# Loading q and k of the first two token groups together: 1 KB packets, a borrowed buffer, and interleaved attention at the start of a fused attention and FFN kernel

## The chip, the cores and the metric

The kernel runs on one core of a Trainium2 chip. A core has five engines that run side by side: TensorE (PE in the profile, with its weight loads as PEld), VectorE (DVE), ScalarE (ACT), GpSimd (POOL) and SyncE (SP), which here mostly issues DMAs. Sixteen DMA engines move data between the chip's main memory and the core's SBUF. PE writes its results to PSUM, from where DVE and ACT copy them to SBUF.

The metric is the device time of one execution in microseconds. The kernel before took 280.76 us, the median of four runs (280.69 to 281.13).

## What is computed

Attention inside chunks of 64 tokens, then a feed-forward block with a squared ReLU. Batch 8, 8 heads, 576 tokens, head dimension 64; so 4608 tokens of width 512, and a hidden width of 2048.

```python
scores = scale * np.matmul(q_c, k_c.transpose(0, 1, 2, 4, 3))   # per 64-token chunk
attn = np.exp(scores - np.max(scores, axis=-1, keepdims=True))
attn = attn / (np.sum(attn, axis=-1, keepdims=True) + 1e-09)
out = np.matmul(attn, v_c)
x = out.transpose(0, 2, 1, 3).reshape(B * S, H * D)
h = np.maximum(x @ w_in, 0.0)
return h * h @ w_out
```

All inputs and the output are float32 in main memory.

## The kernel before

The 4608 tokens are cut into 18 groups of 256, each of four chunks of 64. Two groups make a block of 512 tokens, so there are nine blocks. Attention works on a group, the feed-forward block on a block. The order of all instructions is written out by hand (the scheduler is switched off): each engine executes its instructions in the order in which the Python code emits them, and waits only for data and for free buffers.

One group passes through these steps:

- `qk_pieces` issues the loads of q and k on SP. For the first four groups a partition takes two neighbouring tokens, so one contiguous piece is 2 tokens of 64 floats, 512 bytes. A load of q or k of one group is 512 KB. The tiles `q_sb` and `k_sb` come from a pool of five buffers each.
- `v_pieces` issues the loads of v: even heads to `v_even`, odd heads, shifted by one chunk, to `v_odd`. A contiguous piece is 256 bytes.
- `transpose_qk` (called through `TE` for groups 0 and 1) transposes q and k on PE, 16 transposes each, into a PSUM tile of the pool `ps_ffn`. PE reads only the upper halves of the floats, as bf16. `copy_paired` then copies the tile to `qkT` in SBUF, in two copies: q's on DVE, k's on ACT.
- `scores` (SC) multiplies keys and queries into a PSUM tile of the pool `ps_att`, which has two buffers of two banks, and ACT takes the exponential into `e`.
- `values` (AV) multiplies `e` with v for one tile of 128 tokens at a time, again into a `ps_att` tile. A column of ones in v gives the sums. DVE takes their reciprocal (`rec`) and multiplies (`x`).
- `transpose_x_early` transposes one tile of `x` on PE and copies it to `xT`, on ACT for the first tile of a group of block 0 and on DVE for the second.

The feed-forward block is `ffn_in`, a generator: at each step it multiplies one slice of 128 hidden columns (line 414), ACT applies the ReLU (line 430), and ACT or DVE squares the result into `gT` (lines 440, 442). `gT` is a tile of 128 partitions by 16 slices by 512 tokens in bf16, with one buffer. For block 0 the first four steps work on half a block each: slices 0 and 1 for group 0, then slices 0 and 1 for group 1; from slice 2 on each step takes all 512 tokens. `ffn_out_by_ft` is the second multiplication of block 0.

The weights come in as float32 in 1 KB pieces: `load_w_in` issues the load of one of eight slices of 256 columns on SP and casts it to bf16 on POOL. For slice 0 the casts are three: two on POOL, and one on ACT, which `load_w_in` returns as `cast_rest` to be called later.

`keep_busy(n)` issues matmuls of the identity with itself, n times 128 columns, into a `ps_ffn` tile that nobody reads. It gives PE work while it would wait.

What sets the order at the start is the list of calls from line 633 to line 670: the loads of q and k of groups 0 and 1, then of v of both, then w_in slice 0; then the attention of the two groups, with the first two steps of `ffn_in` placed among the transposes of group 1's `x`; then the other loads of weights and of later groups. From line 672 on a table of slots mixes the attention of later groups into the feed-forward steps of each block.

Of the kernel before, what the change touches and what calls it, by code (L numbers as in the profile page):

```python
# [10 lines left out]
FP32 = mybir.dt.float32  # L11
BF16 = mybir.dt.bfloat16
# [5 lines left out]
def kernel(  # L18
# [9 lines left out]
    nc = tc.nc  # L28

    B, H, S, D = q.shape  # L30
# [4 lines left out]
    n_hp = H // 2  # L35
    n_dt = d_model // 128
    n_ft = d_ff // 128
    GT = 256
# [9 lines left out]
    chunks = whole[:-2] + rest + whole[-2:]  # L48
# [8 lines left out]
    BT = GT * max(len(b) for b in blocks)  # L57
# [5 lines left out]
    att_pool = ctx.enter_context(tc.tile_pool(name="att", bufs=3))  # L63
    ffn_pool = ctx.enter_context(tc.tile_pool(name="ffn", bufs=1))
# [7 lines left out]
    ident = const_pool.tile([128, 128], BF16, name="ident")  # L72
# [17 lines left out]
    def runs(g):  # L90

        for t in range(2):
            (b, s), (b1, s1) = chunks[g][2 * t:2 * t + 2]
            if b == b1:
                yield t, 0, 2 * CH, b, s
            else:
                yield t, 0, CH, b, s
                yield t, CH, CH, b1, s1

    def qk_pieces(g):  # L100
        q_sb = in_pool.tile([128, 2, H, D], FP32, name="q_sb")
# [59 lines left out]
    def go(pieces):  # L161
        for f in pieces:
            f()
# [40 lines left out]
    state = {}  # L204
# [14 lines left out]
    def copy_paired(copy, qkT, psb):  # L219
        src = psb.rearrange("c (h i t p) -> c t h p i", h=n_hp, i=2, t=2)  # L220
        dst = qkT.rearrange("c t h (p i) -> c t h p i", i=2)
        for t in range(2):
            copy(out=dst[:, t], in_=src[:, t])  # L223

    def transpose_qk(g, q_pool, k_pool):
        if ("qkT", g) not in state:
            state["qkT", g] = att_pool.tile(
                [128, 2, 2, n_hp, 128], BF16, name="qkT", bufs=4)
        qkT = state["qkT", g]
        for which, pool in enumerate((q_pool, k_pool)):  # L230
            if pool is None:
                continue
            copy = nc.scalar.copy if which or k_pool is None else nc.vector.tensor_copy
            if pool is ps_ffn:
                bank = pool.tile([128, 512], FP32, name="ps_ffn")
            else:
                bank = pool.tile([128, 1024], FP32, name="ps_att")
            bank = bank.bitcast(BF16)[:, 0:1024]
            transpose_paired(g, which, bank)
            copy_paired(copy, qkT[:, which], bank)  # L240

    def transpose_x_early(g, t):
        j, c = place[g]
# [13 lines left out]
    def keep_busy(n):  # L257
        ps = ps_ffn.tile([128, 512], FP32, name="ps_ffn")
        for k in range(0, n, 4):
            m = min(4, n - k)  # L260
            nc.tensor.matmul(  # L261
                out=ps[:, 0:m * 128], lhsT=ident,
                rhs=ident[:, None, :].to_broadcast([128, m, 128]), start=True, stop=True)
# [105 lines left out]
    def TE(g):  # L369
        transpose_qk(g, ps_ffn, ps_ffn)  # L370
# [253 lines left out]
    def pieces(grps):  # L624
        for g in grps:
            yield from qk_pieces(g)
        for g in grps:
            yield from v_pieces(g)
# [1 line left out]

    first_ffn_in = ffn_in(0, [(0, HT, (0, 1)), (HT, HT, (0, 1)), (0, BT, range(2, n_ft))])

    go(pieces([0, 1]))
    cast_rest = load_w_in(0)
    TE(0)
    keep_busy(8)
    SC(0)
    keep_busy(6)
    TE(1)
    keep_busy(8)  # L640
    SC(1)
    keep_busy(10)
    AV(0, [0])
    keep_busy(4)
    AV(0, [1])
    keep_busy(8)
    transpose_x_early(0, 0)
    keep_busy(10)
    transpose_x_early(0, 1)
    AV(1, [0])  # L650
    keep_busy(8)
    AV(1, [1])
    cast_rest()
    transpose_x_early(1, 0)
    next(first_ffn_in)
    transpose_x_early(1, 1)
    next(first_ffn_in)
    keep_busy(4)

    for i in range(1, 8):  # L660
# [107 lines left out]
```

## Time and profile before

| What | Value |
|---|---|
| median of 4 runs | 280.76 us |
| the profiled execution | 280.71 us |
| its span (first to last instruction) | 278.9 us |
| PE busy | 268.6 us, 96% of the span |
| DVE, ACT, POOL busy | 183.3, 166.4, 47.1 us |
| data read and written in main memory | 36.70 MB, 9.44 MB |
| first matmul of line 414 | 18.74 us |
| start of its unbroken series | 20.23 us |

The profile shows one execution. A line of a group or of the timeline names start, duration, engine, source line, operation, and output and input tiles; in square brackets stands how long the engine was idle before and what ended the wait. The chain that ended last is followed back from the last instruction: at each step to what released it, or to the instruction before it on its engine. A table by windows gives, for each stretch of time, the busy time of each engine (with the number of instructions), then the granted PE clock, the busy share of the DMA engines (several packets in flight on one engine can bring it over 1) and the rate in GB/s. The landing of a DMA is when its completion is seen. The time of an execution is 1.8 us longer than its span.

### The profile page before, as it was taken

The numbers are of one execution on the slowest core, as the hardware profiler recorded it, in microseconds if no ns is written. First come the engines' busy times: TensorE is split into PE (matmuls) and PEld (weight loads), VectorE is DVE, ScalarE is ACT, GpSimd is POOL, SyncE is SP. The second block draws the span as 40 slices with busy tenths as digits, with TensorE's granted clock in tenths as the row PEclk, the third lists the DMA queues.
The fourth block names the chain that finished last, engine by engine and source line by source line (L and its number), as shares of the span: only waits on it lengthen the run. The fifth ranks groups of instructions, "written<-read, shape, count | busy, mean of one in ns | idle before, by whom it ended". The sixth has DMA issues, their size and how long they took to land.

```text
span 278.9 us, 7217 instructions
## 1 busy us (share of the span) xinstructions
PE 268.6 (96%) x2983; PEld 176.8 (63%) x2986; DVE 183.3 (66%) x317; ACT 166.4 (60%) x272; POOL 47.1 (17%) x78
## 2 busy tenths in 40 slices
PE   1999999999999999999999999999999999999995
PEld 1554444788874587448744884488448844884594
DVE  1255705797963795499549954995499549954883
ACT  1458704887348863977297819881978197319720
POOL 2037931432063000000000030003000300051000
PEclk9999999999999999999999999999999999999999
DMA  7999999999999899999999999869699950432003
GB/s 199 243 320 344 362 356 242 302 222 206 214 237 256 204 233 176 248 244 221 179 271 249 181 250 268 191 130 229 183 236 190 254 164 0 79 96 56 0 21 132
DMA packets 143088, 57.09 MB, mean 205 GB/s; under 512 B 110672, under 2 KB 140496, under 8 KB 143056
## 3 DMA queue, kind: packets, MB, share of 16 engines
q1 hardware_dynamic: 140784, 50.15, 78.7%
q0 software_dynamic: 1984, 6.29, 6.6%
q8 instruction: 23, 0.38, 0.6%
q10 hardware_dynamic: 288, 0.20, 0.2%
q14 instruction: 9, 0.07, 0.1%
HBM read 36.70 MB, written 9.44 MB: 165 GB/s over the span
## 4 chain that ended last, share of the span: by engine, by line
PE 91%; DMA 5%; DVE 2%; ACT 0%; issue 0%; SPq 0%; DVEq 0%
PE ps_ffn L414 45%; PE ps_ffn L500 30%; PE ps_ffn L601 4%; DMA xT<-x 3%; PE ps_att L303 2%; PE ps_att L330 2%; DMA k_sb<-in_k_dram 2%; PE ps_ffn L261 1%; PE ps_att L500 1%; PE ps_ffn L214 1%; DVE x L338 1%; PE ps_ffn L249 1%; PE ps_att L214 1%; PE ps_att L357 1%; DVE o_sb L457 0%; ACT qkT L223 0%
## 5 line engine op out<-in xcount | busy, mean ns | idle before, releaser
L414 PE MATMUL ps_ffn<-xT,w_in_bf 128*128 128x512 bf16 (+1 forms) x648 | 129.2, 356 | 0.5 <-DMA xT<-x 0.4
L442 DVE TENSOR_TENSOR gT<-rl 128x512 bf16<-128x512 f32 (+1 forms) x108 | 68.3, 663 | 56.7 <-ACT rl L430 56.4
L414 PEld LDWEIGHTS <-w_in_bf 128*128 128x128 bf16 x648 | 61.7, 98 | 58.5 <-issue 0.6
L430 ACT ACTIVATE rl<-ps_ffn 128x512 f32<-128x512 f32 (+2 forms) x146 | 83.9, 590 | 22.3 <-PE ps_ffn L414 21.4
L500 PEld LDWEIGHTS <-w_st 128*128 128x128 bf16 x664 | 62.8, 98 | 7.1
L395 DVE TENSOR_TENSOR w_st<-gT 128x1536 bf16<-128x1536 bf16 (+2 forms) x75 | 50.2, 719 | 0.8 <-ACT gT L440 0.7
L500 PE MATMUL ps_ffn<-w_out_bf,w_st 128*128 128x256 bf16 x368 | 43.1, 273 | 0.0
L531 POOL DMA_DIRECT2D out_dram<-o_sb x16 | 11.4, 714 | 128.9 <-DVE o_sb L457 126.2
L500 PE MATMUL ps_ffn<-w_sum,w_st 128*128 128x256 bf16 x248 | 28.9, 273 | 0.1
L500 PEld LDWEIGHTS <-gT 128*128 128x128 bf16 x264 | 24.7, 98 | 3.4
L583 ACT COPY o_sb<-ps_ffn 128x512 f32<-128x512 f32 (+1 forms) x8 | 4.5, 558 | 37.4 <-PE ps_ffn L500 37.4
L338 DVE TENSOR_TENSOR x<-ps_att,rec 128x512 bf16<-128x512 f32 x36 | 24.9, 691 | 1.2
L440 ACT ACTIVATE gT<-rl 128x512 bf16<-128x512 f32 (+2 forms) x38 | 23.1, 607 | 1.2
L314 ACT ACTIVATE e<-ps_att 128x1024 bf16<-128x1024 f32 x18 | 17.6, 1024 | 5.7 <-PE ps_att L303 5.7
L500 PE MATMUL ps_ffn<-w_out_bf,gT 128*128 128x256 bf16 x128 | 15.3, 273 | 0.0
L500 PE MATMUL ps_ffn<-w_sum,gT 128*128 128x256 bf16 x120 | 14.6, 273 | 0.0
L601 PE MATMUL ps_ffn<-w_out_bf,gT 128*128 128x512 bf16 x61 | 14.2, 379 | 0.3 <-issue 0.2
L175 POOL CAST w_in_bf<-w_st 128x512 bf16<-128x512 f32 (+2 forms) x12 | 9.7, 829 | 18.1 <-DMA w_st<-in_moe_w_in_dram 18.0
L274 ACT CAST qkb<-k_sb 128x1024 bf16<-128x1024 f32 x10 | 10.5, 1046 | 2.0 <-DMA k_sb<-in_k_dram 2.0
L330 PEld LDWEIGHTS <-e 64*64 64x64 bf16 x576 | 6.5, 107 | 7.1 <-ACT rl L430 2.1
L271 ACT CAST qkb<-q_sb 128x1024 bf16<-128x1024 f32 x10 | 10.5, 1047 | 0.3 <-issue 0.3
L601 PEld LDWEIGHTS <-gT 128*128 128x128 bf16 x64 | 6.0, 98 | 7.0
(59 smaller groups left out, 159.6 us busy)
## 6 DMA issues: line engine op xcount, KB each, us to landing
q_sb<-in_q_dram SPq DMA_DIRECT2D x16, 512.0 KB, 5.7
k_sb<-in_k_dram SPq DMA_DIRECT2D x24, 256.0 KB, 6.0
out_dram<-o_sb POOLq DMA_DIRECT2D x20, 256.0 KB, 4.3
ve_sb<-in_v_dram SPq DMA_DIRECT2D x32, 128.0 KB, 4.1
w_st<-in_moe_w_in_dram SPq DMA_DIRECT2D x8, 512.0 KB, 6.4
w_st<-in_moe_w_out_dram SPq DMA_DIRECT2D x8, 512.0 KB, 5.8
vo_sb<-in_v_dram SPq DMA_DIRECT2D x23, 128.0 KB, 4.2
out_dram<-o_sb SPq DMA_DIRECT2D x9, 256.0 KB, 3.1
```

The lines of the kernel that those rows point to most:

```text
L271: copy(out=qkb[:, 0].rearrange("p (i h d) -> p i h d", i=2, h=H), in_=q_sb.rearrange("p (h i d) -> p i h d", h=H, i=2))
L314: nc.scalar.activation(out=e_out, in_=s_in, func=AF.Exp, scale=scale)
L330: nc.tensor.matmul(out=ps[64 * p:64 * p + 64, a, hp * (D + 1):(hp + 1) * (D + 1)], lhsT=e[64 * c:64 * c + 64, a, hp, t, :], rhs=vb[64 * c: ...
L338: nc.vector.tensor_tensor(out=x[:, t].rearrange("p h a d -> p a h d"), in0=o[:, :, :, 0:D], in1=rec.to_broadcast([128, 2, n_hp, D]), op=AL ...
L395: nc.vector.tensor_tensor(out=state[name, j][:, part], in0=x, in1=y, op=ALU.subtract)
L414: nc.tensor.matmul(out=h[:, n:2 * n] if second else h[:, 0:n], lhsT=w_in_bf[:, dt, ft * 128:(ft + 1) * 128], rhs=xT[:, c // 128:(c + n) // ...
L430: nc.scalar.activation(out=rl, in_=h[:, 0:m], func=AF.Relu)
L440: nc.scalar.activation(out=dst, in_=rl, func=AF.Square)
L442: nc.vector.tensor_tensor(out=dst, in0=rl, in1=rl, op=ALU.mult)
L500: nc.tensor.matmul(out=ps, lhsT=a[:, i, t * 128:(t + 1) * 128], rhs=b[:, i, c:c + n], start=(first and i == 0 and (last or k == 0)), stop= ...
L531: dma.dma_start(out=out[t0:t0 + HT, col:col + HD].rearrange("(t p) d -> p t d", p=128), in_=o_sb.rearrange("p (t d) -> p t d", d=HD))
L601: nc.tensor.matmul(out=o_ps[tt], lhsT=gT[:, ft, tt * 128:(tt + 1) * 128], rhs=w_out_bf[:, ft, :], start=(ft == 0), stop=(ft == n_ft - 1))
```

## The change

Only the start of the kernel changes. Three functions are new: `joint`, `joint_pieces` and `transpose_joint`.

The loads: q of the first 512 tokens (groups 0 and 1 lie in one batch) is loaded in two DMAs of four heads each, then k in the same way. A partition takes four neighbouring tokens, so a contiguous piece is 1 KB. The four DMAs carry 512 KB each, as the four before did. They land in the storage of the first `gT` tile, which is therefore allocated early: its first half holds q, its second half k. The loads of v and of w_in slice 0 follow in the order that they had.

The transposes: `transpose_joint(0)` transposes q of both groups, 32 transposes into one tile of `ps_att` (two banks), and `transpose_joint(1)` k. Each then makes four copies to `qkT`, one per group and tile of 128 tokens: the first tile of a group on DVE, the second on ACT. Each of these copies reads both banks. Numbers of transposes and copies are those of before.

The order of calls: both score steps follow one another, then the values of group 0 and 1, with the first two steps of `ffn_in` moved: the first one now stands ahead of the transposes of both tiles of group 1's `x`, the second between them. The `keep_busy` calls are placed and sized anew, and one now stands before the first transposes.

```diff
+    def joint(which):
+        return gTs[0].rearrange("p f n -> p (f n)")[:, which * 8 * GT * 2:(which + 1) * 8 * GT * 2]
+
+    def joint_pieces():
+        gTs[0] = ffn_pool.tile([128, n_ft, BT], BF16, name="gT")
+        b, s = chunks[0][0]
+        for which, src in enumerate((q, k)):
+            dst = joint(which).bitcast(FP32).rearrange("p (h e) -> p h e", h=H)
+            for hs in (slice(0, H // 2), slice(H // 2, H)):
+                yield lambda dst=dst, src=src, hs=hs: nc.sync.dma_start(
+                    out=dst[:, hs],
+                    in_=src[b, hs, s:s + 2 * GT, :].rearrange("h (s i) d -> s h (i d)", i=4))
...
+    def transpose_joint(which):
+        bank = ps_att.tile([128, 1024], FP32, name="ps_att").bitcast(BF16)
+        src = joint(which).rearrange("p (h i d) -> p h i d", h=H, i=4)
+        dst = bank.rearrange("c (h i q) -> c h i q", h=n_hp, i=4)
+        for hp in range(n_hp):
+            for i in range(4):
+                for a in range(2):
+                    nc.tensor.transpose(
+                        out=dst[64 * a:64 * a + 64, hp, i, :],
+                        in_=src[:, 2 * hp + a, i, 1::2],
+                        identity=ident)
+        parts = bank.rearrange("c (h i r p) -> c r h p i", h=n_hp, i=4, r=4)
+        for g in range(2):
+            if ("qkT", g) not in state:
+                state["qkT", g] = att_pool.tile(
+                    [128, 2, 2, n_hp, 128], BF16, name="qkT", bufs=4)
+            for t, copy in enumerate((nc.vector.tensor_copy, nc.scalar.copy)):
+                copy(
+                    out=state["qkT", g][:, which, t].rearrange("c h (p i) -> c h p i", i=4),
+                    in_=parts[:, 2 * g + t])
...
-    go(pieces([0, 1]))
+    go(joint_pieces())
+    go(v_pieces(0))
+    go(v_pieces(1))
     cast_rest = load_w_in(0)
-    TE(0)
+    keep_busy(20)
+    transpose_joint(0)
+    keep_busy(6)
+    transpose_joint(1)
     keep_busy(8)
     SC(0)
+    keep_busy(4)
+    SC(1)
+    keep_busy(8)
+    AV(0, [0])
+    keep_busy(8)
+    AV(0, [1])
+    transpose_x_early(0, 0)
+    AV(1, [0])
     keep_busy(6)
-    TE(1)
-    keep_busy(8)
-    SC(1)
-    keep_busy(10)
-    AV(0, [0])
-    keep_busy(4)
-    AV(0, [1])
-    keep_busy(8)
-    transpose_x_early(0, 0)
-    keep_busy(10)
     transpose_x_early(0, 1)
-    AV(1, [0])
-    keep_busy(8)
     AV(1, [1])
     cast_rest()
+    keep_busy(4)
+    next(first_ffn_in)
     transpose_x_early(1, 0)
     next(first_ffn_in)
     transpose_x_early(1, 1)
-    next(first_ffn_in)
     keep_busy(4)
```

## The prediction

> **What bounds the kernel now.** I read the page first, then the chain that ended last, then TensorE's idle time, then the first 21 us of the timeline.
>
> ```profile
> span 278.9 us, 7217 instructions
> PE 268.6 (96%) x2983; PEld 176.8 (63%) x2986; DVE 183.3 (66%) x317; ACT 166.4 (60%) x272; POOL 47.1 (17%) x78
> ```
>
> TensorE (PE) is busy for 96% of the span, and the waits place nearly all of its idle time at the two ends: after 20.3 us PE idles 0.16 us at 42.3 us and 0.39 us at 138.3 us, and then until its last matmul not again. So what counts is when the steady matmuls of line 414 begin, and everything behind them moves along.
>
> ```profile
> 18.47 0.40 PE ps_ffn L249 x4
> 18.87 0.48 PE ps_ffn L414 x4
> 19.35 0.36 PE ps_ffn L249 x4
> 19.71 0.44 PE ps_ffn L414 x4
> 20.14 0.22 PE ps_ffn L261
> 20.36 13.00 PE ps_ffn L414 x64
> ```
>
> This is the chain; columns are start, duration, work. The x64 block starts at 20.23 in the timeline: that is the time to beat. It waits for the xT copy on DVE (19.75 to 20.17), and this for the last `x` (18.56 to 19.25). A second branch ends almost together with it: the first slice of w_in.
>
> ```profile
> 18.25 0.42 ACT L175 CAST w_in_bf<-w_st 128x256 bf16<-128x256 f32 x1 [1.35 <-DMA w_st<-in_moe_w_in_dram]
> 18.28 1.00 POOL L175 CAST w_in_bf<-w_st 128x256 bf16<-128x256 f32 x2 [16.09 <-DMA w_st<-in_moe_w_in_dram]
> ...
> 19.73 1.24 POOL L175 CAST w_in_bf<-w_st 128x512 bf16<-128x512 f32 x2 [0.45 <-DMA w_st<-in_moe_w_in_dram]
> ```
>
> The releaser in brackets is the landing of a slice: 18.25, 19.7 and, one cast further in the same view, 21.2, so 1.48 us apart for 512 KB. I call the first landing L. The loads ahead of it are the q and k that the change touches:
>
> ```profile
> L106 SPq DMA_DIRECT2D q_sb<-in_q_dram x2: 444/876/1307, 0.7 to 1.9; - x2
> ...
> DMA to landing us min/median/max: 4.3/5.6/6.8
> ```
> ```profile
> L106 SPq DMA_DIRECT2D k_sb<-in_k_dram x2: 562/1102/1641, 1.2 to 3.2; - x2
> ...
> DMA to landing us min/median/max: 5.6/6.5/7.3
> ```
> ```profile
> 6.00:7.00 1.00, 0.26 (x6) 0.10 (x4) 0.80 (x2) 0.00 (x0) 0.00 (x0) 1.00 1.20 291
> ...
> 11.00:12.00 1.00, 1.00 (x24) 1.00 (x22) 0.48 (x1) 0.00 (x0) 0.00 (x0) 1.00 1.40 193
> ...
> 20.00:21.00 1.00, 1.00 (x10) 0.70 (x8) 0.17 (x1) 0.97 (x4) 0.97 (x2) 1.00 1.10 355
> ```
>
> Issue plus time to landing puts q0, k0, q1, k1 at 5.04, 6.85, 8.66 and 10.5: 1.82 us for each 512 KB. The three windows (last column GB/s) are 512-byte pieces of q and k, 256-byte pieces of v, and 1 KB pieces of w_in, each with the DMA engines full (share at least 1).
>
> **The loads (part 1).** Same bytes, same four issues on SP, ahead of v and w_in as before; 512 descriptors each instead of 1024. SP's issues took 0.44 to 1.64 us only because the queue was full, so I count issue at nothing; if the queue is not what held them, it is 0.44 us at most. The gain in L is the packet size: four loads by 1.82 - 1.48 = 0.34 us is 1.36 us; if the first, which runs while the queue ramps up (324 to 333 GB/s in 3 to 5 us already), gains nothing, 1.02 us. With 324 GB/s in place of 355 it is 7.2 - 6.5 = 0.7 us. I take 1.2, nearest to the landings: L = 17.05. One instruction fetch lies ahead of L too: the window 12 to 13 us has the instruction queue at 7.8% of the 16 engines, 1.25 us of one. PE's instruction count up to there is about the same after, so it stays ahead of L and I leave its cost as it is.
>
> [...]
>
> **Landing of q and k (part 2).** By the same spacing the halves of q land at 4.9 and 6.35, those of k at 7.8 and 9.25. Group 0's k came at 6.85 before, so its scores start later; group 1's came at 10.5, so the pair is earlier. Transposes: 16 took 1.06 us at this stage, 64 before and after. With the first half done early (line 303's x4 before x28 shows that parts of a tile are waited for apart), k's last 16 end at 10.3.
>
> **The copies (part 3).** Eight of 128x512 as before: 0.645 us on DVE, 0.535 on ACT (1.29 and 1.07 for two). Before, each bank had one reader. Now DVE and ACT read the same bank pair in turns. No row shows two engines reading one PSUM tile, so I bound: side by side, k's four end at 11.6; one after another, 2.36 us plus four handovers of 0.05, at 12.83. I take one after another, the safe end; it decides little, as the next part shows.
>
> [...]
>
> **Attention (part 4).** On ACT the exponentials stand behind k's last copy: 12.83 to 13.85 and to 14.87 (1.02 each). PE's queue then: values of group 0 at 13.9 and 14.93; DVE (0.21 + 0.69 each, 0.9 with handovers) ends `x` at 15.2 and 16.15. Group 1's values need v, whose odd tile landed at 16.55 before and so about 15.35; they also wait for the PSUM buffer that `x` frees. `x` of group 1 ends at 17.1, and, after DVE's 0.42 xT copy, at 18.4. Before it was 18.42 and 19.25. From the last `x`, a transpose of 0.40, a copy of 0.42 and handovers make 0.97: 19.37 at the earliest.
>
> **The moved first matmuls (part 5).** The first line 414 piece now precedes group 1's two transposes on PE, and its Relu and Square precede the xT copy on ACT. So both xT copies of group 1 queue behind w_in, which before they did not. From L: ACT cast 0.42 and 0.07, four matmuls 0.61, Relu 0.42, Square 0.37 (start to start), copy 0.58, handovers: L + 2.56. By the other path: POOL's casts to L + 1.03, transposes, second piece 0.43, transpose 0.40, DVE copy 0.42: L + 2.57. Both give 19.6. If L is late, the first line 414 piece holds up on PE both transposes of group 1, on ACT the Relu, the Square and the copy of xT behind its cast, and on DVE the last xT copy; nothing else is queued there before 22 us. The dummy matmuls of line 261 go from 66 to 68 units of 128 columns (0.11 each while slow, 0.055 later); I cost them at nothing because they lie in PE's waits for ACT and DVE, and if the clock is slow that cover is gone (rival B). On POOL, slices 2 to 8 keep their 1.48 us distance, ahead of PE's 1.73 us per slice (8 matmuls at 7.77/36 us from the chain); the w_out loads behind them on SP are then 1.2 us earlier against PE's 0.6.
>
> Sum: start 20.23 - 19.61 = 0.62 earlier. The profiled execution took 280.71 with a span of 278.9, 1.8 around it. So 280.09, and with the median 0.05 above that execution 280.14. gT's storage used for q and k early costs nothing: its first write (19.81 before) comes 8 us after the last transpose.
>
> **Rivals.**
> A. The pieces are not faster. For it: v's 256-byte and q's 512-byte pieces already keep the engines full. Against: 355 GB/s at 1 KB. Start is L + 2.56, so the change breaks even when L moves by 0.58 us; at none it is 281.3.
> B. PE stays at half clock through attention. The PEclk row shows none of it, but two 128x512 dummies took 0.87 at 12.26 and three 0.71 at 13.84: the clock rose near 13 us, after PE had been busy without a long gap from 6.9. Now PE idles until 6.35 except 2.1 us of dummies and 1.06 of transposes, and waits again at 11.2. If it is still slow at 16 us, the dummies ahead of values (0.86 twice, not 0.43) and the values themselves move `x` to 19.8: start 20.8, 281.3. This decides above about 0.6 us of extra PE time between 13.3 and 16. Against it: from 6.35 on the gaps are under 0.4 us.
> C. More comes off: copies side by side, L earlier by 1.36, so the start is 19.4, and the 0.39 us wait at 138 us goes as loads run further ahead: 1.2 in all, 279.5.
> D. PE gets its 0.6 us and a later transfer takes it back: the transposing load of xT that PE waits for at 138 us is issued on SP only at 134.6, behind v loads and another transpose, and took 3.65 us. If these loads keep their old time, PE waits 0.6 us longer there: no change. Against it: SP's issue just before it waits for DVE's and PE's own progress, which moves along.
>
> **Chances.** Forecast (gain 0.3 to 0.9) 0.52, C 0.14, A 0.12, B 0.17, D 0.05. About 0.2%, 0.56 us, is what this measurement tells from no change. Faster by more: two thirds of the forecast's share and all of C, 0.49. Within: the rest of the forecast, half of A, D: 0.28. Slower: B and half of A, 0.23. The likeliest case alone spans 279.9 to 280.45; the range takes C and most of A and B in: 279.4 to 281.4.
>
> **What would show it.** q and k landing at about 1.48 us spacing, the last near 9.25; L near 17.05; ACT and DVE copies of qkT alternating; last `x` near 18.4; the x64 block near 19.6; PE idle after that still about 0.5 us. The prediction fails if L moves by less than 0.6 us, if 128x512 dummies still take 0.43 at 16 us, or if new PE waits of some tenths appear after 20 us.

## The result and the profile after

The kernel after takes 281.70 us (median of 53 runs), the kernel before 280.98 (79 runs on the same chips). The ratio is 1.0022 with a 95% interval of 1.0011 to 1.0033: slower by about 0.6 us, where 0.6 us less was forecast. Times of one kernel differ by about 1 us from chip to chip (280.0 to 281.1 for the kernel before), so below only ratios to the kernel before on the same chip are compared.

The profiled execution took 281.83 us. The head of its page:

```profile
span 280.1 us, 7228 instructions
PE 271.1 (97%) x2983; PEld 178.0 (64%) x2986; DVE 183.2 (65%) x317; ACT 166.5 (59%) x272; POOL 46.8 (17%) x78
```

PE is busy for 2.5 us more than before with as many matmuls on the page (2983), so some of them ran slower. Next the chain of work that ended last, from the landing of k to the unbroken series (start, duration, work; L449 is the matmul that was L414, L296 the dummy of `keep_busy`, L289 the copy of xT):

```profile
2.33 8.22 DMA gT<-in_k_dram
...
10.60 1.08 PE ps_att L263 x16
...
14.41 0.64 PE ps_att L338 x26
15.05 0.97 PE ps_ffn L296 x2
16.02 0.37 PE ps_att L365 x16
16.38 0.97 PE ps_ffn L296 x2
...
20.05 0.60 PE ps_ffn L449 x4
20.64 0.22 PE ps_ffn L284 x4
20.86 0.44 PE ps_ffn L449 x4
21.30 0.24 PE ps_ffn L284 x4
...
21.56 0.43 DVE xT L289
...
22.13 0.92 PE ps_ffn L449 x7
```

The series starts at 22.13 instead of 20.23 (19.61 was forecast). On the path to it stand the landing of k, and two pairs of dummies at 0.97 us each that were costed at nothing. The casts of w_in in the timeline of the kernel after show the landing L:

```profile
17.14 0.98 POOL L189 CAST w_in_bf<-w_st 128x256 bf16<-128x256 f32 x2 [14.96 <-DMA w_st<-in_moe_w_in_dram]
18.72 0.42 ACT L189 CAST w_in_bf<-w_st 128x256 bf16<-128x256 f32 x1
19.48 1.23 POOL L189 CAST w_in_bf<-w_st 128x512 bf16<-128x512 f32 x2 [1.36 <-DMA w_st<-in_moe_w_in_dram]
```

L is 17.14 (forecast 17.05): the loads are faster, though the exact agreement is luck, as the other executions show below. But w_in now waits for others. ACT casts its share only at 18.72, behind the xT copy, and PE starts on it at 20.05. Two one-microsecond windows show the rate (last column, GB/s) of the 1 KB pieces, and that k's last part lost pace in this execution (the DMA share falls from 1.08 to 0.71; it stays under 1 until 15 us, so what lands behind k is late too):

```profile
4.00:5.00 1.00, 0.51 (x11) 0.49 (x12) 0.00 (x0) 0.00 (x0) 0.00 (x0) 1.00 1.08 384
...
10.00:11.00 1.00, 0.40 (x8) 0.40 (x10) 0.00 (x0) 0.00 (x0) 0.00 (x0) 1.00 0.71 153
```

Then PE in the timeline of the kernel after:

```profile
5.82 1.07 PE L263 MATMUL ps_att<-ident,gT 128*64 128x128 bf16 x16 [0.24 <-DMA gT<-in_q_dram]
...
8.94 1.06 PE L263 MATMUL ps_att<-ident,gT 128*64 128x128 bf16 x16 [1.29 <-DMA gT<-in_k_dram]
...
10.60 1.07 PE L263 MATMUL ps_att<-ident,gT 128*64 128x128 bf16 x16 [0.60 <-DMA gT<-in_k_dram]
...
14.98 1.04 PE L296 MATMUL ps_ffn<-ident 128*128 128x512 bf16 x2
...
16.32 1.04 PE L296 MATMUL ps_ffn<-ident 128*128 128x512 bf16 x2
...
18.39 0.50 PE L296 MATMUL ps_ffn<-ident 128*128 128x512 bf16 x2
```

The same pair of dummies takes 1.04 us at 14.98 and at 16.32, and 0.50 at 18.39. PE is at half clock until 18.0, through nearly the whole attention of both groups; before, it rose at 12.8. (The granted clock in the page's row reads full from the start, before its first change too; the durations and the trace's clock events, which all clock times here are taken from, give the change.) After 23 us PE waits for no transfer any more; before, it waited 0.39 us for xT at 138 us (the kernel before's table of waits from 19 us on; columns are total, times, longest):

```profile
PE ps_ffn L414 <- DMA xT<-x: 0.4, 1, 0.4
```

So from the start of the series to the end it takes 257.9 us instead of 258.7.

Two more profiled executions of the kernel after (below) took 280.75 and 280.73 us. In them k lands at 9.6 and the series starts at 21.26 and 21.21: the stall of k at 10 us belongs to the first execution, the half clock to all three (it rises at 18.0, 17.8 and 17.6). Their spans, 278.97 and 278.92 us, equal those of the kernel before (278.93, and 278.90 when it was profiled again): the start is 1.0 us later and the rest 1.0 us shorter. So the profiles show why the start is late; that the kernel as a whole is slower by 0.6 us, and not only with the stall, is shown by the timed runs alone. Among them the second profiled execution of the kernel before lies high (280.68, where the median is 280.00), and these two of the kernel after lie low (medians 280.96 and 281.09).

### The profile page after: what moved, and what is told of

Its sections match the earlier page's. It is cut to its first block, busy times and chain, and to the rows that moved or that the text cites. A ratio compares the mean times of both kernels' runs of the same rounds, so it can differ in the third digit from the quotient of the medians.

```text
span 280.1 us, 7228 instructions
## 1 busy us (share of the span) xinstructions
PE 271.1 (97%) x2983; PEld 178.0 (64%) x2986; DVE 183.2 (65%) x317; ACT 166.5 (59%) x272; POOL 46.8 (17%) x78
## 4 chain that ended last, share of the span: by engine, by line
PE 92%; DVE 3%; DMA 3%; SPq 1%; ACT 0%; issue 0%
PE ps_ffn L449 45%; PE ps_ffn L535 33%; PE ps_ffn L636 4%; DMA gT<-in_k_dram 3%; PE ps_att L365 2%; PE ps_att L338 2%; DVE x L373 1%; PE ps_att L535 1%; PE ps_ffn L296 1%; PE ps_att L228 1%; PE ps_att L392 1%; SPq L110 1%; DVE qkT L273 1%; ACT qkT L273 0%; DVE rec L372 0%
## 5 line engine op out<-in xcount | busy, mean ns | idle before, releaser
L449 PE MATMUL ps_ffn<-xT,w_in_bf 128*128 128x512 bf16 (+1 forms) x648 | 129.2, 356 | 0.7 <-DVE xT L289 0.4
L477 DVE TENSOR_TENSOR gT<-rl 128x512 bf16<-128x512 f32 (+1 forms) x108 | 67.4, 653 | 56.2 <-ACT rl L465 55.8
L449 PEld LDWEIGHTS <-w_in_bf 128*128 128x128 bf16 x648 | 61.9, 98 | 58.6 <-PE ps_ffn L296 0.7
L349 ACT ACTIVATE e<-ps_att 128x1024 bf16<-128x1024 f32 x18 | 17.5, 1024 | 4.5 <-PE ps_att L338 4.5
L372 DVE RECIPROCAL rec<-ps_att 128x8 f32<-128x8 f32 x36 | 7.2, 199 | 6.3 <-PE ps_att L365 6.3
```

The lines of the kernel that those rows point to most:

```text
L349: nc.scalar.activation(out=e_out, in_=s_in, func=AF.Exp, scale=scale)
L449: nc.tensor.matmul(out=h[:, n:2 * n] if second else h[:, 0:n], lhsT=w_in_bf[:, dt, ft * 128:(ft + 1) * 128], rhs=xT[:, c // 128:(c + n) // ...
L477: nc.vector.tensor_tensor(out=dst, in0=rl, in1=rl, op=ALU.mult)
```

## The experiments

The theories in words, with the letters that the expectations use for them (they are not the rivals A to D of the prediction). For the late start: loads of k that land late (L); PSUM copies that take turns (C); the PE clock, through the dummies ahead of the values (P), with gaps in PE's work while it waits for joint q and k, which hold that clock down (P, clock part); for the kernel before, the landing of w_in and v (W). For what follows: the start carries to the end one to one (S); or waits for later transfers take a gain back (G).

All runs in one table. S is the start of the unbroken series, the clock's rise the first of the execution, and the rest is the span less S; these come from one profiled execution, the ratio (to the kernel before on the same chip, 95% interval) from 4 to 12 timed runs (53 for the kernel after).

| Kernel | clock up | S | rest | ratio |
|---|---|---|---|---|
| before | 12.84 | 20.23 | 258.70 | 1 |
| after | 18.01 | 22.13 | 257.92 | 1.0022 (1.0011 to 1.0033) |
| e1 before, start delayed | 11.09 | 21.01 | 257.85 | 1.0042 (1.0018 to 1.0066) |
| e2 no dummies ahead of values | 21.08 | 21.99 | 257.74 | 1.0058 (1.0035 to 1.0080) |
| e3 copies split by bank | 18.04 | 21.95 | 257.93 | 1.0063 (1.0042 to 1.0085) |
| e4 gaps filled | 5.65 | 19.48 | 259.41 | 0.9997 (0.9973 to 1.0022) |
| e5 before again | 12.11 | 20.13 | 258.76 | 0.9998 (0.9984 to 1.0012) |
| e6 after again | 17.78 | 21.26 | 257.71 | 1.0030 (1.0012 to 1.0049) |
| e7 e4, start delayed | 6.28 | 20.89 | 257.80 | 1.0026 (1.0004 to 1.0048) |
| e8 before, gaps filled | 7.34 | 19.89 | 260.52 | 1.0057 (1.0035 to 1.0079) |
| e9 two PSUM tiles | 5.31 | 20.50 | 257.90 | 1.0014 (0.9982 to 1.0046) |
| e10 e4, xT loads first | 5.55 | 20.67 | 260.27 | 1.0026 (0.9997 to 1.0055) |
| e11 before, xT loads first | 10.53 | 19.77 | 259.67 | 1.0011 (0.9981 to 1.0041) |
| e12 e4 and e9, xT loads first | 5.82 | 19.73 | 259.01 | 1.0012 (0.9984 to 1.0040) |
| f1 joint loads alone | 22.29 | 25.85 | 258.06 | 1.0170 (1.0139 to 1.0200) |
| f2 new order alone | 18.07 | 21.95 | 257.82 | 1.0055 (1.0035 to 1.0075) |
| f3 after, third time | 17.57 | 21.21 | 257.71 | 1.0024 (0.9997 to 1.0050) |
| f4 e4 and e9 together | 7.44 | 18.61 | 259.41 | 0.9998 (0.9974 to 1.0022) |

### Does the start carry to the end? Delay it (e1)

The kernel before with 16 more dummy units ahead of the series.

```diff
     next(first_ffn_in)
     keep_busy(4)
+    for _ in range(4):
+        keep_busy(4)
```

> The kernel before, with four more 128x512 dummy matmuls on TensorE directly ahead of the series of first-stage matmuls (0.22 us each at full clock), so that the series starts 0.86 to 0.88 us later and nothing else changes. Theory S (the start carries to the end one to one, as the prediction took it): the time grows by 0.86 us, ratio 1.0031. Theory G (TensorE waits for later transposing loads in the kernel before, 0.39 us at 138 us and some tenths more near 110 us; a later start gives that back): it grows by 0.2 to 0.5 us, ratio 1.0007 to 1.0018, and the wait at 138 us is gone.

S moved from 20.23 to 21.01, but the profiled span stayed (278.86 against 278.93): the wait for xT at 138 us is gone and the rest shrank by 0.85 us. The timed runs are slower by 0.42%, 1.2 us (0.5 to 1.9). The profile shows a later start taking away a later wait; the times show that most of a delay is paid all the same. One profiled execution isn't the mean of twelve: the two are not brought together.

### Are the dummies ahead of the values the cost? (e2)

```diff
     SC(1)
-    keep_busy(8)
     AV(0, [0])
-    keep_busy(8)
     AV(0, [1])
```

> The changed kernel without the two groups of dummy matmuls that stand ahead of the values of group 0 (two times 128x512 each; 0.97 us each in the changed kernel's profile, at half clock). Theory P (TensorE at half clock executes these dummies after their cover is gone, and so they delay the values): the first values start about 15.3 instead of 15.95, the second about 16.3 instead of 17.28, the series starts 0.8 to 1.0 us earlier than 22.1, and the ratio to the kernel before falls from 1.0022 to about 1.000. Theory L (the late landing of k alone is the loss and the dummies lie in waits): the series stays at 22.0 to 22.2 and the ratio at 1.002. If the clock needs these dummies, the clock rises later and the ratio goes above 1.0022.

Slower than the kernel after (1.0058 against 1.0022). Without the two pairs the first `x` starts at 15.16 instead of 15.72 (the third execution of the kernel after, f3 below, where k landed at 9.6 as it did here), but the clock rises only at 21.08, so that everything up to the series runs slow, and S is 21.99 instead of 21.21. The dummies cost time on the path and are needed there: they are dear because of the low clock (1.03 us a pair in f3, 0.50 once it is up), and don't cause it.

### Do the copies' turns matter, and what makes them? (e3)

Each copy is cut by heads, so that DVE reads the first bank of the tile and ACT the second.

```diff
-            for t, copy in enumerate((nc.vector.tensor_copy, nc.scalar.copy)):
-                copy(
-                    out=state["qkT", g][:, which, t].rearrange("c h (p i) -> c h p i", i=4),
-                    in_=parts[:, 2 * g + t])
+            for t in range(2):
+                for half, copy in enumerate((nc.vector.tensor_copy, nc.scalar.copy)):
+                    hs = slice(half * n_hp // 2, (half + 1) * n_hp // 2)
+                    copy(
+                        out=state["qkT", g][:, which, t, hs].rearrange("c h (p i) -> c h p i", i=4),
+                        in_=parts[:, 2 * g + t, hs])
```

> The changed kernel with the copies of the joint transposes cut by heads instead of by tokens: DVE takes the heads in the first PSUM bank, ACT those in the second, so that each bank has one reader; 16 copies of 128x256 instead of 8 of 128x512. Theory C (DVE and ACT taking turns on one bank pair, 2.64 us after the last transpose of k, delays scores and values): the copies run side by side and k's end 1.5 to 1.8 us after its last transpose, the exponentials start 0.8 to 1.1 us earlier, the series starts 0.6 to 1.0 earlier, the ratio is about 1.000. Theory P or L: the copies get shorter but values still stand behind dummies at half clock, so the series starts 0 to 0.4 us earlier, ratio 1.001 to 1.002.

The copies still take turns, now eight short ones. The timeline of this kernel:

```profile
10.75 0.42 DVE L275 COPY qkT<-ps_att 128x256 bf16<-128x256 bf16 x1 [0.82 <-PE ps_att L263]
11.21 0.37 ACT L275 COPY qkT<-ps_att 128x256 bf16<-128x256 bf16 x1 [0.87 <-DVE qkT L275]
...
11.61 0.42 DVE L275 COPY qkT<-ps_att 128x256 bf16<-128x256 bf16 x1 [0.44 <-ACT qkT L275]
12.07 0.37 ACT L275 COPY qkT<-ps_att 128x256 bf16<-128x256 bf16 x1 [0.49 <-DVE qkT L275]
```

Each is released by the other engine's copy, though they read different banks and write different parts. They share a PSUM tile; so the turns don't come with the bank (e9 tries two tiles). From k's transposes the copies take until 14.16, longer than the unsplit ones, and the kernel is 0.3 to 0.4% slower than the one after (1.0063 against 1.0030 on the same chip, 1.0022 over all). k landed at 9.64 here and the clock rose at 18.04 all the same, so a late k isn't what holds the clock.

### Fill PE's gaps (e4)

More dummies before the joint transposes and between their halves, and nothing else.

```diff
+            if hp == n_hp // 2:
+                keep_busy(4 if which else 2)
...
-    keep_busy(20)
+    keep_busy(24)
     transpose_joint(0)
-    keep_busy(6)
+    keep_busy(18)
     transpose_joint(1)
```

> The changed kernel with more dummy matmuls in TensorE's waits for q and k: 24 units of 128 columns instead of 20 ahead of q, 2 between q's halves, 18 instead of 6 ahead of k, 4 between k's halves (0.107 us a unit at half clock; TensorE was idle 0.49, 0.24, 1.29 and 0.60 us there). Theory P, clock part (the idle gaps keep the clock at half until 18 us): the clock rises by 13 to 14.5 us, dummies and values after that take half the time, the series starts 0.6 to 1.0 us earlier, ratio 0.999 to 1.0005. Theory L: the clock rises earlier but the series does not start over 0.3 us earlier, ratio 1.0015 to 1.0025.

PE in the timeline of this kernel (L298 is the dummy, L265 the transpose, L451 the first feed-forward matmul):

```profile
4.50 1.06 PE L265 MATMUL ps_att<-ident,gT 128*64 128x128 bf16 x16
...
5.82 0.64 PE L265 MATMUL ps_att<-ident,gT 128*64 128x128 bf16 x16
...
13.28 0.61 PE L298 MATMUL ps_ffn<-ident 128*128 128x512 bf16 x2
...
14.09 0.60 PE L298 MATMUL ps_ffn<-ident 128*128 128x512 bf16 x2
...
19.48 4.70 PE L451 MATMUL ps_ffn<-xT,w_in_bf 128*128 128x256 bf16 x25 [0.39 <-DVE xT L291]
```

The second 16 transposes already take 0.64 us instead of 1.07, the dummies ahead of the values 0.61 instead of 1.04, and S is 19.48: the forecast 19.61 is reached by filling gaps alone. But the time is 0.9997 of the kernel before, where 0.9978 was forecast (the interval just takes that in), and the table of waits for 90 to 279 us has new ones:

```profile
PE ps_ffn L451 <- DMA xT<-x: 0.7, 2, 0.4
PE ps_ffn L537 <- ACT n L593: 0.3, 1, 0.3
```

PE now waits twice for xT, and once for ACT. The rest took 259.41 us, 1.5 more than in the kernel after and 1.7 more than in its third execution. Matmul by matmul against that execution, counted from S, PE falls behind at these places and nowhere else: 0.3 us at the scores and values of 92 to 95 us, 0.4 and 0.6 at the two waits for xT (109.6 and 138.0), and 0.4 at the one for ACT (216.6). So each wait costs 0.1 to 0.2 us more than its idle time in the table, and these places are the whole 1.7.

### Both kernels again, and the repaired start delayed (e5, e6, e7)

e5 is the kernel before and e6 the kernel after, unchanged. e7 is e4 with 28 more dummy units ahead of the series:

```diff
     keep_busy(4)
+    for _ in range(7):
+        keep_busy(4)
```

> The kernel before, unchanged, as the null of these comparisons and for a second profile of it: ratio 1.000 within the interval. Theory G (the later transposing loads set the end when the series starts early): TensorE again waits for xT, 0.3 us or more in all between 100 and 170 us, with the series started at 19.6 to 20.4. If these waits are absent and the span is then shorter by them, they are a matter of one execution and not of the kernel.

> The changed kernel, unchanged, for its ratio on this chip and a second profile. Theory P (clock): the clock again rises only after 15 us, the series starts at 21.0 to 22.2, ratio 1.002 to 1.006. Theory L (a straggling landing of k): k's last half lands over 10 us again; if it lands near 9.6, as in two of the three variants so far, and the series still starts after 21.3, the late landing was not the cause.

> The kernel with TensorE's early waits filled (the series starts at 19.48 there), with seven more 128x512 dummies ahead of the series: 1.54 us of them, some 0.5 of it in a wait, so that the series starts near 20.5. Theory G: what the earlier start brought was lost to waits for xT later, so delaying it again by 1.0 us costs 0 to 0.4 us: ratio to the kernel before 0.9995 to 1.001. Theory S (the start carries one to one): 1.0 us more than the filled kernel's 0.9997, ratio 1.003 or more.

The kernel before against itself is 0.9998, so 0.14%, the half width of its interval, is about what this comparison can tell; the kernel after is slower again (1.0030). In e7 S is 20.89, 1.41 us later than in e4, and the profiled span is shorter (278.69 against 278.89): no wait over 0.2 us is left after 22 us, and the rest is back at 257.80. By the profiles a start earlier than about 20.9 is given back. By the timed runs e7 is 0.29% slower than e4, with intervals that overlap; one to one it would be 0.50%. So the profiles show the exchange, and the timed runs leave open how much of a delay it pays for.

### Fill the gaps of the kernel before (e8)

```diff
+            if g == 0 and which:
+                keep_busy(6)
             transpose_paired(g, which, bank)
...
     cast_rest = load_w_in(0)
+    keep_busy(28)
     TE(0)
```

> The kernel before with dummies in its own early waits: 28 units of 128 columns ahead of group 0's q and 6 between its q and k transposes, nothing else. The clock then rises at about 5.7 to 9 us instead of 11 to 13. Theory W (w_in and v bind the start of the kernel before, not the clock): the series starts at 19.9 to 20.2 and the ratio is 0.999 to 1.001. Theory P for both kernels: it starts 0.5 us or more earlier, 19.2 to 19.7. With theory G an earlier start does not show in the time.

The clock rose at 7.34 instead of 12.84 and the start came 0.34 us earlier, and the kernel is 0.57% slower. Its table of waits from 23 us on:

```profile
PE ps_att L332 <- DMA vo_sb<-in_v_dram: 0.9, 1, 0.9
PE ps_ffn L502 <- ACT n L558: 0.3, 1, 0.3
```

An early start with the old loads runs into v at 55 us. The rest is 260.52, 1.8 us more than before and 2.8 more than in the third execution of the kernel after. Counted as in e4 against that execution, PE falls behind by 1.2 us at v, 0.2 at the third slice of w_in (22.7 us), 0.3 at the scores and values of 94 to 96, 0.3 at each xT (111 and 139), and 0.5 at the copy on ACT (218).

### Two tiles instead of one (e9)

Each joint transpose goes into two one-bank tiles of `ps_ffn`; DVE copies from the first, ACT from the second.

```diff
-        bank = ps_att.tile([128, 1024], FP32, name="ps_att").bitcast(BF16)
+        banks = [ps_ffn.tile([128, 512], FP32, name="ps_ffn").bitcast(BF16) for _ in range(2)]
...
-                        out=dst[64 * a:64 * a + 64, hp, i, :],
+                        out=dsts[hp // 2][64 * a:64 * a + 64, hp % 2, i, :],
```

> The changed kernel with each joint transpose in two PSUM tiles of one bank each instead of one tile of two banks; DVE copies from the first, ACT from the second, 16 copies of 128x256 (0.42 and 0.37 us each in the kernel with split banks, where they still took turns). Theory C (taking turns was a matter of the tile and cost the start): the copies run side by side, k's end about 1.7 us after its last transpose instead of 2.64, the exponentials start 0.9 us earlier, and the series starts 0.3 to 0.9 us earlier than the 21.3 to 22.1 of the changed kernel; ratio 1.000 to 1.003. Theory P (clock): the clock still rises after 15 us and the series starts no earlier than 20.8; ratio 1.002 to 1.005.

The timeline of this kernel: the two engines' copies of k now lie side by side (they write the same `qkT` tiles as in e3, so it was the PSUM tile that made them take turns), and the exponentials start at 11.36, 2.9 us before those of the kernel after (14.26) and 1.9 us before those of its third execution (13.27).

```profile
8.66 1.42 DVE L275 COPY qkT<-ps_ffn 128x256 bf16<-128x256 bf16 x4 [1.68 <-PE ps_ffn L263]
10.30 1.20 ACT L275 COPY qkT<-ps_ffn 128x256 bf16<-128x256 bf16 x4 [2.64 <-PE ps_ffn L263]
11.36 1.98 ACT L352 ACTIVATE e<-ps_att 128x1024 bf16<-128x1024 f32 x2
...
15.56 0.26 PE L368 MATMUL ps_att<-vo_sb,e 64*64 64x65 bf16 x1 [1.13 <-DMA vo_sb<-in_v_dram]
...
15.91 0.82 PE L299 MATMUL ps_ffn<-ident 128*128 128x512 bf16 x2
```

Of this 1.9 us only 0.7 reaches the start (20.50 against 21.21). PE arrives at group 1's values before v has landed and waits 1.13 us; and the clock, which had risen at 5.31, falls back at 15.55, so that the next dummies take 0.82 instead of 0.60. The same number of dummies as in the kernel after gave an early rise here (5.31, against 17.6 to 18.0): the clock doesn't follow from the instruction list alone.

### Move loads behind the xT transposes (e10, e11, e12)

If waits for xT take the gain back, loads that stand ahead of xT in SP's queue should be moved behind it. e10 does so to e4, e11 to the kernel before, e12 to e4 and e9 together (all with the same edit of the slots of blocks 2 and 3).

```diff
-                go_slots = [*range(6), *range(13, 32)]
+                go_slots = [*range(6), *range(19, 38)]
...
-                go_slots = [*range(16), 23, 24, *range(26, 36)]
+                go_slots = [*range(15), *range(20, 36)]
```

> The kernel with the early waits filled (series at 19.48, waits for xT of 0.7 us after 100 us), and in blocks 2 and 3 the loads of later groups that stood on SP just ahead of the transposing loads of xT moved behind them: one load in block 2, six in block 3. Theory G (these loads take back what the start gained): the waits for xT near 110 and 138 us shrink to under 0.2 us together and the ratio goes below 0.9985. If the waits stay because the queue of the DMA engines as a whole is behind, the ratio stays at 0.9985 to 1.001.

> The kernel before with the same move of loads behind the transposing loads of xT in blocks 2 and 3, its start untouched (series near 20.2, waits for xT of 0.4 us and some tenths more). Theory G: 0.3 to 0.7 us less, ratio 0.9975 to 0.999. If the waits belong to the DMA backlog and not to that order: 0.999 to 1.0005.

> All three together on the changed kernel: early waits filled, two PSUM tiles for each joint transpose, loads behind the transposing loads of xT. Theories P, C and G together: clock up near 6 us, copies of k done near 11.6, series at 18.9 to 19.4, no waits for xT over 0.2 us, ratio 0.995 to 0.998. If the transposing loads still bind, no better than the one-cause kernels: 0.998 to 1.000.

None is faster. The waits for xT are gone in all three; others stand in their place, in e10 from 90 us on:

```profile
PE ps_att L340 <- DMA qkT<-qkb: 1.5, 2, 1.0
```

PE now waits for `qkT`, the transposing loads of q and k. The longer wait (1.0 us at 93 us) isn't the move's doing: its load was issued between 83.1 and 90.7 us, and the first load that stands elsewhere comes only behind the xT loads of 104.5. The shorter one (0.45 us at 120 us) is for a load that moved loads of v now precede. With this one other order the waits change their names and the time stays; that the transfers together, and not their order, have no slack would explain it, but no run here loads less.

### The two halves of the change by themselves (f1, f2), and the kernel after once more (f3)

f1 takes the joint loads and lets the groups follow one another as before; a group's transposes read 64 of the 128 rows, so there are twice as many. f2 keeps the 512-byte loads per group, in the order q0, q1, k0, k1, and takes the new order of everything else.

```diff
-    transpose_joint(0)
-    keep_busy(6)
-    transpose_joint(1)
+    transpose_group(0)
     keep_busy(8)
     SC(0)
...
+    keep_busy(6)
+    transpose_group(1)
```

> One part alone: the joint loads in 1 KB pieces into the first gT, but the attention of the two groups one after another as before, with the dummies and the order of the kernel before; each group's transposes take its 64 partitions of the joint buffer, so they are 32 of 64 rows instead of 16 of 128. If the loads are the gain and the interleaving the loss: w_in lands at 16.9 to 17.4, the series starts at 19.0 to 20.0, ratio 0.998 to 1.000. If group 0 now waits for all of k (landing 9.3 to 10.6 instead of 6.85) and TensorE idles through it, the clock rises after 13 us and the series starts after 20.8, ratio 1.002 to 1.005.

```diff
-    go(joint_pieces())
+    first, second = list(qk_pieces(0)), list(qk_pieces(1))
+    for f in (first[0], second[0], first[1], second[1]):
+        f()
```

> The other part alone: the loads of before (512-byte pieces, q and k tiles of their own, issued q0, q1, k0, k1), and the changed kernel's joint transposes in one PSUM tile, copies in turns, interleaved attention, dummies and order. w_in then lands at 18.2 to 18.5 and k's last quarter at 10.5. The prediction's chain gives w_in + 2.56 = 20.8 at the earliest, as its rival without faster loads said; with a late clock 21.5 to 22.5. Ratio 1.002 to 1.006. A start at or before 20.3 would show that the order itself costs nothing.

> The changed kernel once more, for a third profile: whether the late clock is its habit. Theory P: clock up after 15 us, series at 21.2 to 22.2. If the phase of the clock decides from execution to execution, as the kernel with two PSUM tiles showed (up at 5.3, down at 15.6, up at 19.0), the clock may be up by 6 us here, and the series then starts at 20.0 to 21.0. Ratio 1.002 to 1.004 either way.

f1 is slower by 1.7%: group 0 has to wait for k of both groups (PE idles 3.00 us until 9.56), then the two groups queue one behind the other, and the clock rises at 22.29. f2 is slower by 0.55%: L is 18.50, and the clock rises at 18.07, just as with joint loads. So the new order carries the loss (1.5 us), and within that order the joint loads bring about 0.9 us of it back (1.0055 to 1.0022, whose intervals don't overlap; against the 1.0024 of f3, on the same chip, they do). Neither half is good alone, and the joint loads only lessen what the new order costs.

The third execution of the kernel after, PE in the timeline, shows the prediction's steps without the stall of k:

```profile
9.61 1.06 PE L263 MATMUL ps_att<-ident,gT 128*64 128x128 bf16 x16 [0.58 <-DMA gT<-in_k_dram]
...
14.00 1.03 PE L296 MATMUL ps_ffn<-ident 128*128 128x512 bf16 x2
...
15.33 1.03 PE L296 MATMUL ps_ffn<-ident 128*128 128x512 bf16 x2
...
17.57 0.50 PE L296 MATMUL ps_ffn<-ident 128*128 128x512 bf16 x2
...
21.21 2.98 PE L449 MATMUL ps_ffn<-xT,w_in_bf 128*128 128x256 bf16 x17 [0.39 <-DVE xT L289]
```

### Everything that helped the start, together (f4)

The fillers of e4 and the two tiles of e9, without the moved loads.

```diff
+        banks = [ps_ffn.tile([128, 512], FP32, name="ps_ffn").bitcast(BF16) for _ in range(2)]
...
+            if hp == n_hp // 2:
+                keep_busy(4 if which else 2)
...
-    keep_busy(6)
+    keep_busy(18)
```

> Early waits filled and two PSUM tiles for each joint transpose, the later loads where they were: the best start that the runs point to. Clock up by 6 us, series at 19.0 to 19.6. Theory G (behind a start before about 20.8 the loads decide): span 278.4 to 279.0 all the same, ratio 0.998 to 1.001. Theory S (the start carries): 1.0 us faster than before, ratio 0.9965.

S is 18.61, 1.6 us earlier than before, and the time is the same as before (0.9998). Its waits from 20 us on:

```profile
PE ps_ffn L454 <- POOL w_in_bf L189: 1.1, 1, 1.1
```

PE reaches the third slice of w_in before it has landed and been cast, and 1.1 us go there at once. That is not the early start alone: the first three slices land at 16.05, 18.15 and 21.83 here, 2.1 and 3.7 us apart instead of 1.5. No kernel of this study is faster than the one before by more than the measurement tells.

### What sets the clock's rise

The trace's clock events have a spacing: in e9 they stand at 5.31, 15.55 and 18.96 us, so 10.24 (three times 3.41) and 3.41 apart. From the rise to the next event, the fall behind the last matmul, it is 266.24 us in the kernel before and 262.83 in the kernel after, 78 and 77 times 3.413. So I cut each execution into stretches of 3.41 us that end with its rise. The tables by windows (first PE column: busy us of 3.41), the kernel before:

```profile
6.01:9.43 3.42, 2.67 (x49) 1.39 (x49) 1.29 (x2) 1.07 (x2) 0.00 (x0) 1.00 1.20 289
9.43:12.84 3.41, 3.41 (x60) 2.10 (x48) 1.29 (x2) 1.50 (x2) 0.00 (x0) 1.00 1.39 216
```

and the kernel after:

```profile
4.36:7.77 3.41, 2.89 (x34) 1.78 (x34) 0.69 (x1) 0.12 (x1) 0.00 (x0) 1.00 1.01 348
7.77:11.18 3.41, 1.64 (x28) 1.41 (x30) 0.69 (x1) 1.05 (x2) 0.00 (x0) 1.00 0.95 221
11.18:14.60 3.42, 2.97 (x61) 1.38 (x59) 1.38 (x2) 1.41 (x3) 0.00 (x0) 1.00 0.75 171
14.60:18.01 3.41, 3.41 (x72) 1.52 (x64) 1.10 (x3) 1.60 (x2) 0.86 (x2) 1.00 1.04 327
```

Before, the stretch up to 12.84 is the first that PE fills: group 0's transposes and scores, with the dummies, cover the wait for group 1's q and k. After, both wait for the same q and k, so 0.4 to 1.8 us are idle in each stretch until both groups have all they need, and the first filled one ends at 18.01. In 17 of the 18 executions the clock rose at the end of the first stretch that PE filled to 94% or more, or (e9) to 85%; stretches of 87% in the kernel after didn't do. f1 is the exception: two stretches filled to 100% with much work on half the rows went by before it rose. With the new order, all five executions with fillers in the gaps (e4, e7, e10, e12, f4) have the rise by 7.5 us; of the seven without, six have it at 17.5 us or later, and e9 alone early. The phase of these stretches doesn't seem to be the kernel's own: with the same kernel the rise differs by some tenths (18.0, 17.8, 17.6).

That a filled stretch brings the rise is read off these executions alone. In e9 the clock fell after a stretch that wasn't idle, with PE busy for 2.09 of 3.42 us and no gap over 1.13; what made it fall was not shown.

## Why the prediction was wrong

**Loads (part 1): right, and the size too small.** L was forecast at 17.05; the three executions have 17.14, 15.97 and 15.91, against 18.25 before. That the first comes so near is luck: there the DMA engines lost pace from 9 to 15 us (shares of 0.63 to 0.97, against 1.05 to 1.34 in the third). The other two gained 2.3 us, not 1.2. And the instruction fetch did not stay ahead of L, as the step assumed: its 16 KB packet runs from 12.9 to 14.1 us before, and from 16.1 to 17.1, 14.7 to 16.1 and 14.7 to 15.9 after, so up to L or past it. The second slice then lands 2.3 to 2.5 us after the first instead of 1.5 (POOL in the timeline of the third execution):

```profile
15.91 0.99 POOL L189 CAST w_in_bf<-w_st 128x256 bf16<-128x256 f32 x2 [13.72 <-DMA w_st<-in_moe_w_in_dram]
18.32 1.22 POOL L189 CAST w_in_bf<-w_st 128x512 bf16<-128x512 f32 x2 [1.42 <-DMA w_st<-in_moe_w_in_dram]
```

By the second slice (19.73 before, 18.42 and 18.32 in these two) the gain is 1.3 and 1.4 us, near the step's own upper bound of 1.36. That the fetch now holds up the second slice and not the first would explain why L gained more; no run keeps the fetch in its place to show it. Rival A, loads that aren't faster, falls: from 3 to 8 us the 512-byte pieces moved 305 GB/s on average (289 to 333 in single microseconds), the 1 KB pieces 356, 336 and 344 in the three executions. SP's four issues of q and k took 0.46 to 0.51 us each, against 0.44 to 1.64 before; that a full queue held the longer ones, as the step took it, was not shown.

**Landings (part 2): right but for one execution.** q at 4.5 and 5.8 (forecast 4.9 and 6.35), k at 8.0 and 9.6 in the third execution (7.8 and 9.25), at 8.9 and 10.6 in the first.

**Copies (part 3): right.** In turns, 2.66 us for k's four in the third execution (2.56 forecast). (Its 10.3 and 2.56 make 12.86, not 12.83, which changes nothing.) The step's remark that "it decides little" was wrong: in e9 the exponentials came 1.9 us and the start 0.7 us earlier; with the gaps filled the start gained 0.9 by it (e4 to f4, where L was 0.6 earlier too).

**Attention (part 4): this step failed.** It put the values at 13.9 and 14.93 and the end of the last `x` at 18.4; the third execution has the values at 14.96 and 16.30 and the last `x` done at 19.82. The failing assumption stands in part 5: that dummies "lie in PE's waits" and cost nothing. At half clock a pair takes 1.03 and stands between the scores and the values, twice. That is rival B, to which 0.17 was given, and by its numbers: "moves `x` to 19.8", 281.3 us or 1.0019 of before, where 19.82 and 1.0022 were measured. The argument against B was that gaps from 6.35 us on would be under 0.4 us. They were 0.2 to 0.6 in the third execution (1.3 at most in the first), and anyway it is not the length of a gap that counts in these traces but whether a whole 3.41 us is filled (so in 17 of the 18 executions, e9 with 85%). e4 shows the cause: with the gaps filled, values, `x` and start come where the forecast had them.

**From the last `x` to the start (part 5): mis-sized.** 0.97 was forecast; it is 1.39 in the kernel after, in the third execution and in e4 alike. The second piece of line 449 (0.43) now lies between the two transposes, on this path and not only on the one from L. The path from L was sized right: in f4, where PE waits for the cast of w_in, the start is 18.61 = L (16.05) + 2.56, the very sum of the prediction.

**Start to end "one to one": the second step that failed.** It was to carry 0.62 us. Where the start came earlier than before and the later loads kept their places (e4, f4, and e8 with the old loads), the rest took 259.4 to 260.5 us instead of 258.7, and no time was gained; where it came at 20.5 or later, with these loads in place, the rest was 257.7 to 258.1. In the timed runs f4 and e8 decide it: one to one they would be at 0.9942 and 0.9988, outside their intervals. e4's interval reaches 0.9973, which is one to one there, so e4 alone would not. So what was rival D, at 0.05, is the rule here for an earlier start: a later transfer takes it back. The name that D gave to the transfer, xT at 138 us, is right for e4; with xT served first it is the transposing loads of q and k, with a still earlier start w_in, which landed late in that one execution. C's part that the xT wait would go came true, but because PE arrives later, not because the loads run ahead.

Of the distance between forecast (0.9978) and result (1.0022), 1.2 us, the filled gaps give back about 0.7 (to 0.9997), the first failed step; the remaining 0.5 is the second. Both have the half width of e4's interval on them, 0.7 us.

What stays open: how much of an early start is paid back on average, as e7 and e1 grew more in the timed runs than in their profiles, and the 0.6 us that the kernel after loses in the timed runs is not in its second and third profile; why k's last part lost pace in one execution; and why f1's clock stayed low over two filled stretches.

## What to carry to other kernels

Joining the loads made the transfers faster here and made everything wait for the last of them: look at what the split loads let PE do meanwhile, because here that work also brought the clock up at 12.84 us instead of 18.01. Read what a dummy or any other filler costs from the stage's own clock, by the duration of one known instruction there (here a pair of dummies, 1.04 us and then 0.50), and ask whether PE is busy throughout a stretch as long as the one that counted here (3.41 us, in 17 of the 18 executions) rather than how long its gaps are. And before a gain at the start is carried to the end, look whether the transfers behind it have slack: a start earlier than the loads could follow returned as waits here (1.7 us in e4).

## What the runs showed that was not expected

- Two engines' copies from one PSUM tile took turns even where they read different banks of it (e3: 0.42 and 0.37 us alternating); from two tiles they ran side by side (e9: 1.42 on DVE and 1.20 on ACT for four). In these kernels the tile is the unit of that order.
- The clock fell back in the middle of attention after a stretch of 3.41 us with PE busy for 2.09 (e9), while stretches of 2.13 in e4 (9.06 to 12.47 us) and of 1.92 in e9 itself (5.31 to 8.72) left it up.
- Filling the gaps of the kernel before made the clock rise 5.5 us earlier and the kernel 0.57% slower (e8).
